# FNet mixing plus PEER experts on one Trainium2 core: the symmetry compares of the expert part on GpSimd, first column group in halves, its rows 0 in a tile of their own

## The chip, the cores and the metric

The kernel runs on one core of one Trainium2 chip. A core has five engines with a queue of instructions each, worked off in order: TensorE (PE in the profile; PEld are its weight loads), VectorE (DVE), ScalarE (ACT), GpSimd (POOL) and SyncE (SP), which here only issues transfers. Engines wait for each other by semaphores. The metric is the device time of one launch in microseconds; the number compared is the median of several runs.

## What is computed

The input x has 2048 rows of 512. It is normalized by row, and three things are added: x, a Fourier mixing by dense DFT matrices, and a layer of product-key experts (32 heads, two of 4096 experts for each head and row).

```python
xn = _layernorm(x, axis=-1)
return x + _A_ref(xn, A_dft_seq_re, ...) + _B_ref(xn, B_w_q, B_k1, B_k2, B_u, B_v)
# _A_ref
a = jnp.einsum("bsd,ed->bse", x, dft_hid_re)
b = jnp.einsum("bsd,ed->bse", x, dft_hid_im)
y = jnp.einsum("ts,bse->bte", dft_seq_re, a) - jnp.einsum("ts,bse->bte", dft_seq_im, b)
# _B_ref
s1 = jnp.einsum("nhd,ed->nhe", q1, k1)      # 64 scores; the same with q2, k2
...                                         # two best of each half, two best of the four sums
act = _gelu(jnp.einsum("nd,nhkd->nhk", xf, ue))
out = jnp.einsum("nhk,nhk,nhkd->nd", g, act, ve)
```

The DFT matrices are ordinary inputs. The kernel uses their symmetries to do a fraction of the Fourier work, so it has to establish on the chip that the matrices it was given have them. If they had not, a general path at the end of the program would compute the result anew; with these inputs it is skipped.

## The kernel before

**Stages.** The first 90 us or so fold x and do the short Fourier product. Until about 460 us the scores of 32 heads are computed, sixteen blocks of 128 rows for each group of four heads (`scores`, L796), and VectorE picks the two best (L804, L808). From about 470 us on runs the *expert part*, in which all 4096 experts are computed for 14 of the 16 blocks as dense products: u times x for every expert (`u_part`, L956), Gelu on ScalarE (L959), multiplication by a matrix of gates that is built on TensorE from two one-hot matrices (`g_mm`: VectorE makes L and R in L980, L988 and L991, TensorE multiplies them in L993; `w_part`: L1004, L1011, L1014), and the product with v (`v_part`, L1023). The last two blocks are done by gathering rows instead: `fetch` gathers one u row and one v row per partition (L1049, issued by GpSimd), `dot` multiplies on VectorE (L1065), `gain` scales on ScalarE (L1075 to L1078) and adds on GpSimd (L1083).

**The block loop.** For block b, TensorE does eight groups (cg) of twelve v matmuls into one PSUM bank `v`; `finish` (L1038, VectorE) reads that bank and adds the row block `y` to it; then TensorE does the eight groups of u matmuls of block b + 2, 48 each. Groups 2 and 5 of them use the PSUM buffers with the tag "pc", of which there are two; one of them holds `px`, which the gather part reads all the time, the other is `v`. So group 2 of u cannot start before `finish` has read `v`. `y` is loaded by SyncE (L1031), and x is added to it by an accumulating transfer that GpSimd issues (L1032), both traced at group 4 of the v loop (`add_x`).

**The compares.** `compare(n)` deals with one tile of one DFT matrix: 64 of them, n = 32 ri + 8 g + kk for the real or imaginary matrix ri, the column group g and a part kk of the matrix's other axis. The tile `cx` has 128 rows (partitions), one for each column of the matrix that belongs to the group, and in each row four quarters of 256 elements that should agree up to sign. `diff` subtracts the first quarter from the others (L752, for all column groups but the first), and then compares the first quarter's halves (mirror, L758, L760). In the first column group, g = 0, row 0 is its own mirror image and has other values, so there `diff` works with three operations that leave row 0 out by a factor `not0` (L739, L741), and treats row 0 in single-row operations (L743, L758 on one row, L766, L768). `judge`, on ScalarE, sums the absolute differences into a column of `chk` and the absolute values of the first quarter's part into a column of `asum` (L778, L780). 28 tiles, those of `EARLY`, are compared during the scores, with `diff` on GpSimd; 36 run in the expert part with `diff` on VectorE: the 16 tiles of g = 0, and 20 others. `compare_w` does the same for four tiles of the hidden DFT matrix (L1121 to L1144, VectorE), and `fit` checks ranges of other inputs (ScalarE). `verdict` at the end reduces `chk` and `asum` over rows.

**What sets the order.** The program is written out without loops, and each engine's queue follows the order of the text nearly throughout. `paced` is called once for each group of the v and u loops; called with odd cg it lets the list `units` (40 entries) advance evenly over the loop. An entry issues its loads at once; `after(2, work)` puts `diff` two paced steps later and `judge` two more, and `hold` adds an order without a semaphore behind the matmuls of that step. `pick` distributes the gather work in the same way. The tiles of the compares take turns with those of `w_part`, `fit` and others in four buffers (tag "w").

Of the kernel before, what the change touches and what calls it, by code (L numbers as in the profile page):

```python
# [8 lines left out]
F32 = mybir.dt.float32  # L9
# [6 lines left out]
AF = mybir.ActivationFunctionType  # L16
# [3 lines left out]
P = 128  # L20
# [16 lines left out]
def tile_fnet_peer(ctx, tc, x, ca, cb, c5, wt, wf, wr, wq, kt, ut, vn, uv, out):  # L37
# [54 lines left out]
    NF = NW + 32 + NCH - 1  # L92
    EARLY = [*range(8, 24), *range(40, 52)]
    early = cst.tile([P, len(EARLY)], F32, name="early")
    sums_sb = cst.tile([P, 138 + NF + 3], F32, name="sums")
    chk, asum = sums_sb[:, 0:70], sums_sb[:, 70:138]


    wsc = cst.tile([P, 5], F32, name="wsc")
    sw, sk, smx, inv1 = wsc[:, 0:1], wsc[:, 1:2], wsc[:, 2:3], wsc[:, 3:4]  # L100
    k16 = sums_sb[:, 0:128].bitcast(F16).rearrange("p (l w k) -> p l w k", l=2, w=2)
    fits = sums_sb[:, 138:]
# [453 lines left out]
    def part_b(safe, stS, stP, stE, xt, u_sb, cmp_p):  # L556
# [163 lines left out]
        def compare(n, at=None):  # L720
# [11 lines left out]
            nc.sync.dma_start(tf[:, P:], cb[ri, g, kk].rearrange("p b c -> p (b c)"))  # L732
            sgn = (((1, 1, 1), (-1, 1, -1)), ((-1, -1, 1), (1, -1, -1)))[ri][odd]
            ops = [ALU.subtract if v > 0 else ALU.add for v in sgn]
            op = ops[1]

            def diff():
                if g == 0:
                    nc.vector.tensor_tensor(tv[:, 1], tv[:, 1], tv[:, 0], op=ops[0])  # L739
                    for i in (2, 3):  # L740
                        nc.vector.scalar_tensor_tensor(tv[:, i], tv[:, 0], not0, tv[:, i], op0=ALU.mult, op1=ops[i - 1])  # L741
                    f = (-1 if ri else 1) * sgn[1] * sgn[2]
                    nc.vector.tensor_tensor(tv[0:1, 3], tv[0:1, 3], tv[0:1, 2],  # L743
                                            op=ALU.subtract if f > 0 else ALU.add)
                else:
                    sets = {}
                    for i, o in enumerate(ops):
                        sets.setdefault(o, []).append(i + 1)
                    for o, ix in sets.items():
                        sl = slice(ix[0], ix[-1] + 1, ix[1] - ix[0] if len(ix) > 1 else 1)  # L750
                        v = tv[:, sl]
                        v_eng.tensor_tensor(v, v, tv[:, 0:1].to_broadcast([P, len(ix), 256]), op=o)  # L752
                m = ALU.add if ri else ALU.subtract

                def mirror(v):

                    c = 0 if kk else 1
                    v_eng.tensor_tensor(v[:, 2:4, c:], v[:, 2:4, c:], v[:, 0:2, c:], op=m)  # L758
# [12 lines left out]
                mirror(t[:, 0])  # L771
                if kk == 0:
                    v_eng.memset(t[:, 0, 2, 0:1], 0.0)
# [321 lines left out]
        def pick(after, k=1):  # L1095
            done[0] += k
            made = nc.cur_bb.bb.instructions
            for f in picks[done[1]:-(-len(picks) * done[0] // turns)]:
# [3 lines left out]
                for i in made[first:]:  # L1102
                    if i.engine in (mybir.EngineType.DVE, mybir.EngineType.Activation):
                        follow(i, after)
                    if i.engine == mybir.EngineType.Activation and after.ins.name in GL:
                        follow(i, GL[after.ins.name])

        def compare_w(n):


# [24 lines left out]
                nc.vector.memset(r[:, 255:256], 0.0)  # L1135
            nc.vector.scalar_tensor_tensor(v[2], v[0], not0, v[2], op0=ALU.mult, op1=op)
            if ri:
                nc.scalar.activation(v[0][0:1, 0:P], v[0][0:1, 0:P], AF.Abs, accum_out=chk[0:1, 68 + half:69 + half])
# [5 lines left out]
            after(2, lambda: nc.scalar.activation(f, f, AF.Abs, accum_out=chk[:, n:n + 1]))  # L1144

        def fit(n):

# [14 lines left out]
        def verdict():  # L1162
# [1 line left out]


            N = NF + 3
            fm = sums_sb[:, 138 + NF:]
# [3 lines left out]
            cols = ((slice(0, 64), 50), (slice(64, 70), 47))  # L1171
            for i, (c, k) in enumerate(cols):
                nc.vector.tensor_reduce(fa[:, i:i + 1], asum[:, c.start:min(c.stop, 68)], axis=AX.X, op=ALU.add)
# [6 lines left out]
            k = nc.gpsimd.partition_all_reduce(fr[:, 2:], sums_sb[:, 138:], P, bass_isa.ReduceOp.absmax)  # L1180
# [21 lines left out]
            NW + k, *range(2 * k, min(2 * k + 2, NW)), NW + 16 + k)]  # L1202
        todo_n = [n for n in range(68) if n not in EARLY]
        units = [lambda n=n: (compare if n < 64 else compare_w)(n) for n in todo_n]
        streams = [[fit_units, 0, 0], [units, 0, 0]]

        def flush(mm):
# [11 lines left out]
                st[2] += 1  # L1219

        if not safe:
            nc.vector.memset(chk[:, 68:70], 0.0)
# [237 lines left out]
```

## Time and profile before

| | us |
|---|---|
| median of 3 runs | 1118.81 |
| lowest and highest | 1116.66, 1120.2 |
| the profiled execution, its own time | 1113.87 |
| its span in the trace | 1112.1 |

A row of the profile that groups instructions reads: line, engine, operation, what is written and from what (names of the program's tiles), shapes as partitions x elements and type, how often; then the busy time in us and the mean of one in ns; then the time that the engine stood idle just before these, and what ended it. Rows of a timeline begin with the start and the length in us; a bracket gives the idle time before and who ended it. A row of waits gives the total in us, how many times, and the longest. A row of windows gives the stretch, its length, for each engine the busy time and the number of instructions, the granted clock of TensorE (1.00 is full), the share of the transfer engines and GB/s.

### The profile page before, as it was taken

The page shows a single profiled execution, that of the slowest core. Times are in us where ns is not written, and L with a number is a line of the kernel's source. Part 1 is how long each engine was busy: PE and PEld are TensorE (multiplying, and loading weights), DVE is VectorE, ACT ScalarE, POOL GpSimd, SP SyncE. Part 2 cuts the span into 40 slices and gives each one's busy share as a digit, 9 for nine tenths or more (in the row PEclk, how much of TensorE's full clock was granted, in tenths as well). Part 3 has the DMA queues.
Part 4 walks back from the last instruction along what each step waited for, and adds up shares of the span by engine and source line. Part 5 has one row for each costly group of instructions (what it writes and reads, how often), then busy time and mean ns, then how long its engine had stood idle before and what let it go on. Part 6 is the DMA issues. An engine that isn't in the chain of part 4 may idle for free. (4 is left out here: it accounts for less than half of the span.)

```text
span 1112.1 us, 28462 instructions
## 1 busy us (share of the span) xinstructions
PE 1070.3 (96%) x11070; PEld 700.6 (63%) x11070; DVE 996.7 (90%) x2786; ACT 717.7 (65%) x1324; POOL 640.3 (58%) x552
## 2 busy tenths in 40 slices
PE   5899999999999999999999999999998999999897
PEld 4355555454544544987695776968667686786853
DVE  6978897978999999987999999999999999998981
ACT  3576657778788767423766667767566666765660
POOL 0013537588797855211668677756666667667651
PEclk9899999999999999999999999999998999999899
DMA  8248153535446332553677577676767567776521
GB/s 326 83 172 284 49 198 113 173 125 198 153 153 206 106 114 65 186 158 109 186 213 238 193 212 231 225 232 201 215 199 209 182 214 237 230 222 189 158 67 51
DMA packets 84433, 196.72 MB, mean 177 GB/s; under 512 B 10294, under 2 KB 27069, under 8 KB 84288
## 3 DMA queue, kind: packets, MB, share of 16 engines
q1 hardware_dynamic: 63394, 123.49, 33.1%
q0 software_dynamic: 20736, 71.31, 21.8%
q8 instruction: 88, 1.44, 0.5%
q14 instruction: 57, 0.47, 0.1%
q10 hardware_dynamic: 158, 0.01, 0.0%
HBM read 177.68 MB, written 17.10 MB: 175 GB/s over the span
## 5 line engine op out<-in xcount | busy, mean ns | idle before, releaser
L796 PE MATMUL s<-m,xq 128*128 128x512 f16 x1536 | 338.9, 379 | 0.0
L956 PE MATMUL z<-xb,u 128*128 128x128 f16 x5376 | 313.9, 221 | 15.5 <-DVE y L1038 15.5
L956 PEld LDWEIGHTS <-u 128*128 128x128 f16 x5376 | 307.6, 99 | 19.2 <-issue 16.4
L1083 POOL TENSOR_TENSOR ov<-ov,ga 128x512 f32<-128x512 f32 x128 | 203.5, 1590 | 167.2 <-ACT ga L1078 145.7
L1023 PE MATMUL v<-v,act 128*128 128x512 f16 x1344 | 298.6, 379 | 0.0
L796 PEld LDWEIGHTS <-xq 128*128 128x128 f16 x1536 | 148.3, 98 | 171.4 <-issue 0.2
L1023 PEld LDWEIGHTS <-act 128*128 128x128 f16 x1344 | 128.3, 98 | 146.1
L1049 POOL DMA_INDIRECT ga<-in_uv_dram,eix x128 | 173.0, 1351 | 47.2 <-POOL ov L1083 34.2
L980 DVE TENSOR_TENSOR L<-io_lam,cmp 128x2048 f16<-128x2048 f16 x112 | 157.8, 1441 | 13.5 <-PE g L993 13.5
L804 DVE MAX8 vals<-ss 128x8 f32<-128x64 f32 x1024 | 152.4, 216 | 14.1 <-ACT ss L801 14.0
L959 ACT ACTIVATE act<-z,scl 128x512 f32<-128x512 f32 x112 | 75.8, 679 | 97.2 <-PE z L956 96.3
L808 DVE FIND_INDEX8 idx<-vals,ss 128x8 uint16<-128x256 f32 x256 | 107.1, 418 | 0.0
L801 ACT ACTIVATE ss<-s,wsc 128x512 f32<-128x512 f32 x112 | 75.5, 680 | 43.4 <-PE s L796 33.7
L1011 ACT ACTIVATE act<-w 128x1024 f16<-128x1024 f32 x56 | 75.5, 1348 | 43.3 <-DVE w L1004 39.8
L1078 ACT ACTIVATE ga<-ga,za 128x512 f32<-128x512 f32 x128 | 92.1, 721 | 9.8 <-ACT za L1076 0.4
L1014 DVE TENSOR_TENSOR act<-w,act 128x1024 f16<-128x1024 f32 x56 | 86.1, 1539 | 6.7 <-ACT act L1011 5.8
L778 ACT ACTIVATE cx<-cx 128x896 f32<-128x896 f32 x64 | 60.6, 946 | 40.3 <-DVE cx L758 12.9
L1065 DVE SCALAR_TENSOR_TENSOR ga<-ga,px 128x512 f32<-128x512 f32 x128 | 85.6, 676 | 0.1
L1004 DVE SCALAR_TENSOR_TENSOR w<-act,scl,g 128x1024 f32<-128x1024 f32 x56 | 70.9, 1271 | 0.4 <-ACT act L959 0.2
L169 POOL TENSOR_TENSOR wq<-wq,wh 128x1024 f16<-128x1024 f32 x26 | 55.4, 2134 | 24.4 <-ACT wq L166 23.7
L993 PEld LDWEIGHTS <-L 128*128 128x128 f16 x1792 | 52.2, 96 | 9.5 <-issue 2.7
L993 PE MATMUL g<-R,L 128*128 128x32 f16 x1792 | 54.0, 176 | 2.2 <-DVE w L1004 1.9
(274 smaller groups left out, 1312.4 us busy)
## 6 DMA issues: line engine op xcount, KB each, us to landing
cx<-in_cb_dram SPq DMA_DIRECT2D x64, 448.0 KB, 4.6
wq<-in_wq_dram SPq DMA_DIRECT2D x32, 512.0 KB, 5.8
fit<-in_wq_dram SPq DMA_DIRECT2D x28, 512.0 KB, 5.4
uv<-in_ut_dram SPq DMA_DIRECT2D x16, 512.0 KB, 4.1
uv<-in_vn_dram SPq DMA_DIRECT2D x16, 512.0 KB, 3.5
xq<-in_x_dram SPq DMA_DIRECT2D x8, 512.0 KB
xt_d<-xq SPq DMA_DIRECT2D x16, 256.0 KB, 3.0
cx<-in_ca_dram SPq DMA_DIRECT2D x64, 64.0 KB, 2.8
```

The costliest lines, as they stand in the source:

```text
L796: mm = nc.tensor.matmul(ps, xt[i][:, l, kd, :], m[:, r, kd, :], start=(n == 0), stop=(n == 3 * KD - 1))
L804: nc.vector.max(vals[:, i, w, :, h], s[:, g, :])
L808: nc.vector.max_index(idx[:, i, w].rearrange("p k h -> p (k h)"), vals[:, i, w, 0:2].rearrange("p k h -> p (k h)"), s[:, w * HC:g + 1, :]. ...
L956: mm = nc.tensor.matmul(p[:, cc * P:(cc + 1) * P], ug[:, l, c % 2, kd, :], xb[:, r, kd, :], start=(n == 0), stop=(n == 3 * KD - 1))
L980: nc.vector.tensor_tensor(L.rearrange("p t (l two) -> p t l two", two=2), io_lam.rearrange("p (l two) -> p l two", two=2).unsqueeze(1).to_ ...
L993: i = nc.tensor.matmul(p[:, hf, t * NC:(t + 1) * NC], L[:, t, :], R[:, hf * 16 + t, :], start=True, stop=True)
L1014: nc.vector.tensor_tensor(w16[..., 1], w, w16[..., 0], op=ALU.subtract)
L1023: mm = nc.tensor.matmul(pv, w16[:, c, :, l], vg[:, r, c % 2, :], start=(c == 0 and k == 0), stop=(c == NC - 1 and k == 2))
L1049: nc.gpsimd.indirect_dma_start(out=t, out_offset=None, in_=uv, in_offset=bass.IndirectOffsetOnAxis(ap=eix[:, n].rearrange("p k h -> p (k h ...
L1065: nc.vector.scalar_tensor_tensor(t, t, 1.0, T["x"], op0=ALU.mult, op1=ALU.mult, accum_out=T["z", n][:, s:s + 1])
L1078: nc.scalar.activation(t, t, AF.Copy, scale=z)
L1083: T["a"] = nc.gpsimd.tensor_tensor(o, o, t, op=ALU.add)
```

## The change

`diff` of the 36 tiles in the expert part goes to GpSimd, except for tiles 0 and 32 (g = 0, kk = 0), which stay as they are. To treat the other 14 tiles of g = 0 like all others, row 0 must not be in them: they are loaded in two halves, rows 1 to 64 into partitions 0 to 63 and rows 64 to 127 into partitions 64 to 127, so row 64 stands in them twice. Each half is two transfers, as the whole was. The rows 0 of these 14 tiles are compared in a new tile, `compare_r`, the third entry of `units`: GpSimd clears it, eight small transfers put 3 or 4 rows each at partitions 0, 32, 64 and 96, VectorE does three operations for each of these four places and a copy or a memset where the sign rules want it, and ScalarE judges it into a new column of `chk`. `chk` grows from 70 to 71 columns, with the columns behind it moved by one. The pace of the 41 entries is that of the 40 before, within a step.

```diff
-    sums_sb = cst.tile([P, 138 + NF + 3], F32, name="sums")
-    chk, asum = sums_sb[:, 0:70], sums_sb[:, 70:138]
+    sums_sb = cst.tile([P, 139 + NF + 3], F32, name="sums")
+    chk, asum = sums_sb[:, 0:71], sums_sb[:, 71:139]
...
-            v_eng = nc.vector if at is None else nc.gpsimd
+            v_eng = nc.vector if n % 32 == 0 else nc.gpsimd
             tf = t.rearrange("p s q c -> p (s q c)")
             tv = t.rearrange("p s q c -> p s (q c)")
-            nc.sync.dma_start(tf[:, :P], ca[ri, g, :, kk * P:(kk + 1) * P])
-            nc.sync.dma_start(tf[:, P:], cb[ri, g, kk].rearrange("p b c -> p (b c)"))
+            own = g == 0 and kk == 0
+            half = ((slice(0, 64), slice(1, 65)), (slice(64, P), slice(64, P)))
+            for e, a in half if g == 0 and kk else ((slice(0, P),) * 2,):
+                nc.sync.dma_start(tf[e, :P], ca[ri, g, a, kk * P:(kk + 1) * P])
+                nc.sync.dma_start(tf[e, P:], cb[ri, g, kk, a].rearrange("p b c -> p (b c)"))
...
             def diff():
-                if g == 0:
+                if own:
...
-                if g == 0:
+                if own:
                     mirror(t[0:1, 2])
...
+        def compare_r(n):
+            t = bp.tile([P, 4, 4, 64], F32, tag="w", name="cx_r", bufs=WB)
+            tf = t.rearrange("p s q c -> p (s q c)")
+            tv = t.rearrange("p s q c -> p s (q c)")
+            nc.gpsimd.memset(tf, 0.0)
+            cls = []
+            for c in range(4):
+                ri, odd = divmod(c, 2)
+                k0, k1 = (4, 8) if odd else (1, 4)
+                e = slice(32 * c, 32 * c + k1 - k0)
+                nc.sync.dma_start(tf[e, :P], ca[ri, 0, 0:1, k0 * P:k1 * P].rearrange("o (k f) -> (o k) f", f=P))
+                nc.sync.dma_start(tf[e, P:], cb[ri, 0, k0:k1, 0:1].rearrange("k o b c -> (k o) (b c)"))
+                cls.append((ri, odd, e))
+            def work():
+                for ri, odd, e in cls:
+                    sgn = (((1, 1, 1), (-1, 1, -1)), ((-1, -1, 1), (1, -1, -1)))[ri][odd]
+                    f = (-1 if ri else 1) * sgn[1] * sgn[2]
+                    m = ALU.add if ri else ALU.subtract
+                    nc.vector.tensor_tensor(tv[e, 1], tv[e, 1], tv[e, 0], op=ALU.subtract if sgn[0] > 0 else ALU.add)
+                    nc.vector.tensor_tensor(tv[e, 3], tv[e, 3], tv[e, 2], op=ALU.subtract if f > 0 else ALU.add)
+                    nc.vector.tensor_tensor(t[e, 0::2, 2:4], t[e, 0::2, 2:4], t[e, 0::2, 0:2], op=m)
+                    if odd and ri:
+                        nc.vector.tensor_copy(t[e, 2, 0:2], t[e, 0, 0:2])
+                    elif odd == ri:
+                        nc.vector.memset(t[e, 2, 0:2], 0.0)
+                after(2, lambda: nc.scalar.activation(tf[:, P:], tf[:, P:], AF.Abs, accum_out=chk[:, n:n + 1]))
+            after(2, work)
...
         units = [lambda n=n: (compare if n < 64 else compare_w)(n) for n in todo_n]
+        units.insert(2, lambda: compare_r(64))
```

More of the change, by code (lines that the diff above doesn't have):

```diff
@@ L101, in tile_fnet_peer @@
     k16 = sums_sb[:, 0:128].bitcast(F16).rearrange("p (l w k) -> p l w k", l=2, w=2)
-    fits = sums_sb[:, 138:]
+    fits = sums_sb[:, 139:]
     hoff = cst.tile([P, HC], F32, name="hoff")
@@ L1137, in compare_w @@
             if ri:
-                nc.scalar.activation(v[0][0:1, 0:P], v[0][0:1, 0:P], AF.Abs, accum_out=chk[0:1, 68 + half:69 + half])
+                nc.scalar.activation(v[0][0:1, 0:P], v[0][0:1, 0:P], AF.Abs, accum_out=chk[0:1, 69 + half:70 + half])
             c = P - half
@@ L1143, in compare_w @@
             f = t.rearrange("p k e -> p (k e)")[:, P - half * ri:]
-            after(2, lambda: nc.scalar.activation(f, f, AF.Abs, accum_out=chk[:, n:n + 1]))
+            after(2, lambda: nc.scalar.activation(f, f, AF.Abs, accum_out=chk[:, n + 1:n + 2]))
         def fit(n):
@@ L1166, in verdict @@
             N = NF + 3
-            fm = sums_sb[:, 138 + NF:]
+            fm = sums_sb[:, 139 + NF:]
             fa = bp.tile([P, 2], F32, tag="fa", name="fa", bufs=1)
@@ L1170, in verdict @@
             o = bp.tile([1, 8], F32, tag="ok", name="ok", bufs=1)
-            cols = ((slice(0, 64), 50), (slice(64, 70), 47))
-            for i, (c, k) in enumerate(cols):
-                nc.vector.tensor_reduce(fa[:, i:i + 1], asum[:, c.start:min(c.stop, 68)], axis=AX.X, op=ALU.add)
+            cols = ((slice(0, 65), 50), (slice(65, 71), 47))
+            for i, c in enumerate((slice(0, 64), slice(64, 68))):
+                nc.vector.tensor_reduce(fa[:, i:i + 1], asum[:, c], axis=AX.X, op=ALU.add)
             nc.vector.tensor_scalar(bnd, bnd, -31.5, None, op0=ALU.add)
@@ L1179, in verdict @@
             follow(i.ins, T["a"])
[L1180 removed]
+            k = nc.gpsimd.partition_all_reduce(fr[:, 2:], sums_sb[:, 139:], P, bass_isa.ReduceOp.absmax)
             follow(k.ins, i)
@@ L1221, in part_b @@
         if not safe:
-            nc.vector.memset(chk[:, 68:70], 0.0)
+            nc.vector.memset(chk[:, 69:71], 0.0)
             for k in range(0, len(EARLY), 16):
```

## The prediction

> **What bounds the kernel now.** I read the page first, then one window over the expert part, TensorE's waits, and the timelines at the places where TensorE stands still.
>
> ```profile
> span 1112.1 us, 28462 instructions
> PE 1070.3 (96%) x11070; PEld 700.6 (63%) x11070; DVE 996.7 (90%) x2786; ACT 717.7 (65%) x1324; POOL 640.3 (58%) x552
> ```
>
> TensorE is busy for 96% of the span, so nothing can be worth more than its holes. The change touches only the expert part, from 525 us on:
>
> ```profile
> core 0: us, PE busy (x) PEld busy (x) DVE busy (x) ACT busy (x) POOL busy (x), PEclk, DMA share, GB/s
> 525.00:1112.00 587.00, 563.10 (x7202) 414.35 (x7199) 539.03 (x782) 378.80 (x805) 379.10 (x265) 0.98 0.64 195
> ```
>
> There VectorE has 48 us free of 587, GpSimd 208. TensorE's waits in that part, by who ended them:
>
> ```profile
> PE z L956 <- DVE y L1038: 15.5, 6, 4.8
> PE g L993 <- DVE w L1004: 1.9, 1, 1.9
> ```
>
> All 17.4 us wait for VectorE, 15.5 of them for L1038, which drains the finished v bank. The third u group of the next block (cg 2, line 946) takes that bank, so L1038 has the first two groups, 96 matmuls or 5.52 us, as its cover. Four of the six holes, each with its length in the bracket, and the 96 matmuls ahead of one:
>
> ```profile
> 613.45 1.72 PE L956 MATMUL z<-xb,u 128*128 128x128 f16 x28 [2.71 <-DVE y L1038]
> ...
> 798.40 0.77 PE L956 MATMUL z<-xb,u 128*128 128x128 f16 x11 [2.67 <-DVE y L1038]
> ...
> 839.90 5.52 PE L956 MATMUL z<-xb,u 128*128 128x128 f16 x96
> 849.38 0.91 PE L956 MATMUL z<-xb,u 128*128 128x128 f16 x7 [3.96 <-DVE y L1038]
> ...
> 1040.08 1.22 PE L956 MATMUL z<-xb,u 128*128 128x128 f16 x10 [4.84 <-DVE y L1038]
> ```
>
> These are 14.18 us; the other two share the last 1.3. A hole costs twice, because the granted clock falls behind it (length, busy time and matmuls, clock):
>
> ```profile
> 840.69:847.52 6.83, 4.73 (x85) 1.00 0.64 181
> 847.52:854.35 6.83, 4.97 (x48) 0.50 0.59 193
> 799.74:803.15 3.41, 3.41 (x58) 0.50 0.65 177
> 1038.67:1045.50 6.83, 5.42 (x60) 0.50 0.59 184
> ```
>
> At full clock 85 matmuls took 4.73 us, 18.0 per us; behind the hole at 845 the 48 took 4.97 instead of 48/18.0 = 2.67, so 2.30 us are lost. The same sum gives 2.1 at 1038 and, at half speed, about 1.7 at 799. The holes and their echoes together are 17.4 + 6.1 = 23.5 us: the most this change can bring.
>
> What stood ahead of L1038 on VectorE at two of them:
>
> ```profile
> 607.98 1.50 DVE L739 TENSOR_TENSOR cx<-cx 128x256 f32<-128x256 f32 x1
> 609.40 0.91 DVE L741 SCALAR_TENSOR_TENSOR cx<-cx,not 128x256 f32<-128x256 f32 x2
> 611.18 1.55 DVE L758 TENSOR_TENSOR cx<-cx 128x128 f32<-128x128 f32 x2
> ...
> 841.42 3.29 DVE L980 TENSOR_TENSOR L<-io_lam,cmp 128x2048 f16<-128x2048 f16 x2
> 844.64 1.50 DVE L739 TENSOR_TENSOR cx<-cx 128x256 f32<-128x256 f32 x1
> 846.06 2.60 DVE L741 SCALAR_TENSOR_TENSOR cx<-cx,not 128x256 f32<-128x256 f32 x2
> 848.59 0.74 DVE L1038 SCALAR_TENSOR_TENSOR y<-v,scl,y 128x512 f32<-128x512 f32 x1
> ```
>
> In both it is a first-group compare (L739 to L758), which the change moves. Note the two L741: 0.91 us at 609, 2.60 at 846. The longer one met an add on GpSimd; the two engines hold each other up.
>
> **The change part by part.**
>
> *What VectorE loses.* Its compare rows in the window, all shapes together:
>
> ```profile
> L752 DVE TENSOR_TENSOR cx<-cx 128x512 f32<-128x512 f32 (+2 forms) x36 | 31.2, 902 | 3.5 <-DMA cx<-in_cb_dram 3.5
> L758 DVE TENSOR_TENSOR cx<-cx 128x128 f32<-128x128 f32 (+3 forms) x52 | 29.6, 592 | 0.1
> L741 DVE SCALAR_TENSOR_TENSOR cx<-cx,not 128x256 f32<-128x256 f32 x32 | 19.8, 659 | 0.0
> L739 DVE TENSOR_TENSOR cx<-cx 128x256 f32<-128x256 f32 x16 | 12.5, 781 | 0.0
> L743 DVE TENSOR_TENSOR cx<-cx 1x256 f32<-1x256 f32 x16 | 10.0, 623 | 0.0
> ```
>
> That is 103.1 us in 36 tiles. Tiles 0 and 32 stay on VectorE: each keeps one L739, two L741, one L743 and two L758, 0.78 + 1.32 + 0.62 + 1.18 = 3.9, so 7.8 in all. The new row tile adds 12 tensor operations on 3 or 4 rows of 256 elements plus a copy and a memset; nothing in the trace starts at row 32 or 64, the nearest row is L743, so 12 x 0.62 = 7.5 and some 1 us more. The bounds are nothing (all of it fits into the 48 free us) and 12 x (0.62 + 1.27), 23 us, if each meets one GpSimd add. I take 8.5: it runs once, near the start, and no hole lies there. Net VectorE is relieved of 103.1 - 7.8 - 8.5 = 87 us.
>
> *What GpSimd gains.* 34 tiles: seven with one 768-element difference (tiles 1 to 3 and 24 to 27), 27 with one of 512 and one of 256, and the mirror of 128 in each. GpSimd did the same shapes in the first half:
>
> ```profile
> L752 POOL TENSOR_TENSOR cx<-cx 128x512 f32<-128x512 f32 x20 | 25.5, 1274 | 2.8 <-DMA cx<-in_cb_dram 2.8
> L752 POOL TENSOR_TENSOR cx<-cx 128x256 f32<-128x256 f32 x20 | 14.7, 734 | 0.0
> L752 POOL TENSOR_TENSOR cx<-cx 128x768 f32<-128x768 f32 x8 | 14.6, 1822 | 0.0
> L758 POOL TENSOR_TENSOR cx<-cx 128x128 f32<-128x128 f32 x24 | 10.9, 456 | 8.2 <-issue 6.9
> ...
> L1083 POOL TENSOR_TENSOR ov<-ov,ga 128x512 f32<-128x512 f32 x127 | 202.2, 1592 | 145.1 <-ACT ga L1078 123.6 <-ACT za L1075 6.8 <-DVE act L1014 5.9
> ```
>
> 7 x 1.82 + 27 x 2.01 + 34 x 0.46 = 82.6 us, and a memset of the row tile, which no row shows (between nothing and the 1.82 of the widest compare). GpSimd goes from 379 to some 463 of 587. It has the room: L1083 alone waits 145.1 us, nearly all for ScalarE.
>
> *What the stalls do.* Each us of arithmetic on GpSimd makes VectorE wait somewhere. The big operation ahead of L1038 shows how much:
>
> ```profile
> L980 DVE TENSOR_TENSOR L<-io_lam,cmp 128x2048 f16<-128x2048 f16 x93 | 134.0, 1475 | 4.0 <-PE g L993 4.0
> ...
> L980 DVE TENSOR_TENSOR L<-io_lam,cmp x93: 1197/1211/2876, 524.2 to 1072.7; 128x2048 f16<-128x2048 f16 x93
> ```
>
> Its median is 1.211 us, its mean 1.475; so 0.26 us of each is waiting, 24 us in all, against 127 adds of 1.27, 161 us of GpSimd arithmetic: 0.15 us per us. Another 82.6 add 12 us, 0.13 per L980, of which two stand ahead of each L1038. L1038 itself reads PSUM and is never held. The bounds at one boundary are nothing, and a whole compare, 1.27 + 0.73 + 0.46 = 2.46. I take 0.3 at each of six boundaries that have no margin, +1.8, with 2.46 x 6 = 14.8 as the upper end.
>
> The Trainium skill, SBUF — State Buffer, section Who interferes with whom, says that the two engines share one port pair, which whoever starts first holds for its whole instruction while the other stands still. The 2.60 against 0.91 of L741 agrees; by that rule alone the sum would lie between my two bounds, since it doesn't say how often they meet.
>
> *Halved loads.* Fourteen tiles are loaded by four transfers instead of two, and the row tile by eight: 36 more issues on SyncE.
>
> ```profile
> L732 SPq DMA_DIRECT2D cx<-in_cb_dram x34: 422/426/2416, 539.9 to 995.3; - x34
> cx<-in_cb_dram SPq DMA_DIRECT2D x64, 448.0 KB, 4.6
> ```
>
> 36 x 0.43 = 15 us of issuing over the whole part, at most 0.86 per tile ahead of the next y or xb load; the bytes grow by one row in 128. The load lands in 4.6 us and the compare is traced two paced steps after it, two u groups, 5.5 us, so it is covered; without that cover GpSimd, no longer VectorE, waits. I take nothing; the upper end is 15 us on a queue that has slack.
>
> The Trainium skill, DMA: Bandwidth & Descriptors, section Rules for kernel authors, advises against two transfers to disjoint halves, because they serialize. If that cost a second landing, the load would take 9.2 us and GpSimd would wait some 3.7 us per first-group tile; no row of this profile shows a halved load, and the sum here leaves it out.
>
> *ScalarE* gets one judge more among 805 instructions, and in place of VectorE waits for GpSimd's compare; two steps lie between the two in the code.
>
> **The sum.** The profiled execution took 1113.87 us, span 1112.1 and 1.8 around it. At 613 the removed operations, 3.96 us, cover the hole of 2.71; at 849 the removed 1.50 + 2.60 cover 3.96 and the 2.30 behind it: 8.97. At 798 no compare stands right ahead, but VectorE comes to that hole with no pause, and 87 us less work lets it come earlier; I take half of 2.67 + 1.7, 2.2. The hole at 1040 belongs to the weight compares (compare_w), which stay: nothing. Less 1.8 for stalls: 8.97 + 2.2 - 1.8 = 9.4. So 1113.9 - 9.4 = 1104.5 for a run like the profiled one. The three runs have a median of 1118.81, 4.9 above the profiled; against that I forecast **1109.4 us**.
>
> **The rivals.**
>
> *Everything closes.* If the lighter VectorE also reaches L1038 in time at 798 and 1040, up to 23.5 us go: 1095. Against it: the hole at 1040 has its own cause.
>
> *The engines only trade waits: no change.* The lock takes back what the move gives. If all of VectorE's compare time above its unhindered length were to reappear on L980 and its kin at the boundaries, 0.3 would become 1.5 at six boundaries, 9 us, and eat the 9.4: 1118.4. For it: VectorE and GpSimd were both stretched; against it: the compares, 87 us of the work that GpSimd's adds now run into, are gone from VectorE. The Trainium skill, Perfetto Trace Analysis, section Optimizing Scalar/DVE Operations, says that moving work between these two might not help for this reason; the 2.60 is the trace's witness for it.
>
> *y comes late: slower.* L1038 needs y, and the x part of y is added by a transfer that GpSimd's queue issues (L1032), in order, behind the compares now.
>
> ```profile
> 555.39 1.00 POOL L1032 DMA_DIRECT2D y<-in_x_dram  x1
> 564.24 0.75 DVE L1038 SCALAR_TENSOR_TENSOR y<-v,scl,y 128x512 f32<-128x512 f32 x1 [1.52 <-issue]
> 836.47 1.01 POOL L1032 DMA_DIRECT2D y<-in_x_dram  x1
> ...
> DMA to landing us min/median/max: 4.9/5.9/8.8
> ```
>
> The last row is L1032's. At 564 VectorE stood idle 1.52 us although v was done: y took 8.8 us to land and one small hole is due to it. At 836.47 + 5.9 + 0.74 the bank would be free at 843.1, and TensorE needs it at 839.90 + 5.52 = 845.4: 2.3 us of margin, less than one compare of 2.46. If two compares (4.9) stand ahead of L1032, that boundary has a hole of 2.6 and the one at 564 grows by 4.9. As an estimate, 1.5 us at each of twelve boundaries and two more half-clock echoes of 2.3 make 22.6, against 9.4 won: +13, 1132. It decides from the point where GpSimd runs over 2.3 us behind its order. For it: GpSimd at 79% busy; against it: its idle time is spread over all adds, so it rarely queues two compares.
>
> **How the numbers follow.** Forecast 0.50, everything closes 0.12, trade of waits 0.17, late y 0.21. About 0.3%, 3.4 us, is what a measurement tells from no change; the forecast's own range (9.4, less up to 13 more of stalls, or 4 more won) is 1105 to 1118, of which a little lies within 0.3%, and late y has a part there too. So faster 0.60, same 0.18, slower 0.22. The range leaves out the end of the first rival and the upper half of the last: 1098 to 1127.
>
> **What would show it.** Right: L752 and L758 on GpSimd in the expert part, VectorE's busy time in the window near 455 to 500, and the waits of TensorE for L1038 at about 8 us with the hole at 1040 still there. Wrong: VectorE idle ahead of L1038 with y the last to come (late y); L980's mean above 1.7 us with the holes unchanged (trade); ScalarE waiting for GpSimd's L758 with TensorE behind it, which I gave no price.

## The result, and the profile after

The changed kernel took 1130.57 us (median of four runs, 1129.88 to 1136.34), beside 1118.49 for the kernel before: a ratio of 1.0131, 95% interval 1.009 to 1.0172. It is 12 us slower; 9 us faster was forecast. The profiled execution took 1130.87 us against 1113.87; that one of before lies 4.6 us under its median, so the two traces are 17.0 us apart where the medians are 12.1. The lines of the changed kernel are three higher than before: L956 is now L959, L980 L983, L988 L991, L991 L994, L1014 L1017, L1038 L1041, L752 L755, L758 L761, L778 L781, L1083 L1086.

The page, and the window over the expert part (its columns as before):

```profile
span 1129.1 us, 28514 instructions
...
PE 1072.7 (95%) x11070; PEld 701.8 (62%) x11070; DVE 971.3 (86%) x2649; ACT 718.5 (64%) x1326; POOL 734.7 (65%) x652
```

```profile
525.00:1129.00 604.00, 567.35 (x7215) 416.70 (x7212) 516.78 (x645) 379.38 (x807) 474.25 (x365) 0.98 0.62 190
```

The window is 17.0 us longer, which is the whole difference of the two spans. TensorE is busy 4.3 us longer for the same matmuls of the program (567.35 against 563.10; the mean granted clock of the execution was 0.982 against 0.987) and idle 12.8 us longer. Who ended the waits of TensorE, ScalarE and VectorE there:

```profile
PE z L959 <- DVE y L1041: 21.5, 8, 6.3
PE g L996 <- DVE w L1007: 5.2, 1, 5.2
PE z L959 <- DVE cx L776: 3.1, 1, 3.1
PE z L959 <- ACT act L962: 0.5, 1, 0.5
...
ACT cx L781 <- POOL cx L761: 78.7, 24, 7.4
...
ACT cx_r L1138 <- DVE cx_r L1135: 9.9, 1, 9.9
...
DVE R L991 <- ACT cmp L699: 19.5, 8, 5.3
```

TensorE's 17.4 us have become 30.3, and most of it is still the wait for `finish`, L1041. VectorE, with fewer instructions, reaches it later. Two things are new. ScalarE stands 78.7 us at `judge` (L781) for GpSimd's mirror (L761), where it stood 28.1 us for VectorE's compares before, and 9.9 us at the judge of the row tile. What stands behind the judge in ScalarE's queue is late too: VectorE waits 19.5 us for L699, where it waited 3.5 before. The second is in the groups of the same window:

```profile
L1086 POOL TENSOR_TENSOR ov<-ov,ga 128x512 f32<-128x512 f32 x127 | 190.0, 1496 | 63.8 <-ACT ga L1081 43.0 <-DVE R L991 8.3 <-DVE L L983 6.6
...
L983 DVE TENSOR_TENSOR L<-io_lam,cmp 128x2048 f16<-128x2048 f16 x93 | 145.9, 1608 | 8.2 <-PE g L996 8.1
L1017 DVE TENSOR_TENSOR act<-w,act 128x1024 f16<-128x1024 f32 x49 | 95.1, 1943 | 13.2 <-ACT act L1014 11.3 <-ACT za L1078 1.9
L755 POOL TENSOR_TENSOR cx<-cx 128x512 f32<-128x512 f32 (+2 forms) x61 | 79.3, 1315 | 0.6
...
L991 DVE TENSOR_TENSOR R<-io_c,cmp 128x1024 f16<-128x1024 f16 x46 | 58.6, 1274 | 19.5 <-ACT cmp L699 19.5
L994 DVE TENSOR_TENSOR R<-R,cmp 128x1024 f16<-128x1024 f16 x46 | 48.2, 1049 | 1.3
...
L761 POOL TENSOR_TENSOR cx<-cx 128x128 f32<-128x128 f32 (+1 forms) x34 | 31.7, 933 | 2.3
L1041 DVE SCALAR_TENSOR_TENSOR y<-v,scl,y 128x512 f32<-128x512 f32 x13 | 9.6, 742 | 16.6 <-PE v L1026 16.4 <-issue 0.2
```

The kernel before had, beside the 134.0 us of L980 that the prediction shows:

```profile
L1014 DVE TENSOR_TENSOR act<-w,act 128x1024 f16<-128x1024 f32 x49 | 76.8, 1569 | 5.1 <-ACT act L1011 4.3 <-ACT za L1075 0.8
L991 DVE TENSOR_TENSOR R<-R,cmp 128x1024 f16<-128x1024 f16 x46 | 41.0, 891 | 1.2
L988 DVE TENSOR_TENSOR R<-io_c,cmp 128x1024 f16<-128x1024 f16 x46 | 38.9, 845 | 3.5 <-ACT cmp L699 3.5
```

The same 234 operations of VectorE, all with two inputs from SBUF, took 290.7 us before and take 347.8 now: 57.1 us more. Those whose second input lies in PSUM did not change: L1007 takes 1274 ns (1268 before), L1068 679 (676), L1041 742 (740). On GpSimd the compares take 79.3 + 31.7 = 111.0 us, and all its two-input work went from 202.2 to 301.0, by 98.8. So each us of it that was added stretched these four groups by 0.58 us.

The longest hole, at 565, in the timeline:

```profile
559.62 5.52 PE L959 MATMUL z<-xb,u 128*128 128x128 f16 x96
...
560.85 2.72 DVE L1132 TENSOR_TENSOR cx_r<-cx_r 4x256 f32<-4x256 f32 x1
561.45 1.83 POOL L755 TENSOR_TENSOR cx<-cx 128x768 f32<-128x768 f32 x1
...
563.60 1.50 DVE L1017 TENSOR_TENSOR act<-w,act 128x1024 f16<-128x1024 f32 x1
...
566.57 2.36 DVE L983 TENSOR_TENSOR L<-io_lam,cmp 128x2048 f16<-128x2048 f16 x2
566.62 0.95 ACT L1138 ACTIVATE cx_r<-cx_r 128x896 f32<-128x896 f32 x1 [9.93 <-DVE cx_r L1135]
...
570.64 0.74 DVE L1041 SCALAR_TENSOR_TENSOR y<-v,scl,y 128x512 f32<-128x512 f32 x1
571.44 0.80 PE L959 MATMUL z<-xb,u 128*128 128x128 f16 x6 [6.30 <-DVE y L1041]
```

VectorE works on the row tile ahead of L1041. One of its operations, on four rows, takes 2.72 us while GpSimd does a compare of 1.83; ScalarE stands 9.93 us at the row tile's judge.

### The profile page after: what moved, and what is told of

Read it like the earlier page. It is cut to its first block, busy times and chain, and to the rows that moved or that the text cites. A ratio compares the mean times of both kernels' runs of the same rounds, so it can differ in the third digit from the quotient of the medians.

```text
span 1129.1 us, 28514 instructions
## 1 busy us (share of the span) xinstructions
PE 1072.7 (95%) x11070; PEld 701.8 (62%) x11070; DVE 971.3 (86%) x2649; ACT 718.5 (64%) x1326; POOL 734.7 (65%) x652
## 5 line engine op out<-in xcount | busy, mean ns | idle before, releaser
L959 PE MATMUL z<-xb,u 128*128 128x128 f16 x5376 | 315.4, 221 | 25.1 <-DVE y L1041 21.5
L959 PEld LDWEIGHTS <-u 128*128 128x128 f16 x5376 | 308.6, 99 | 29.2 <-issue 26.3
L1026 PE MATMUL v<-v,act 128*128 128x512 f16 x1344 | 301.0, 381 | 0.0
L1086 POOL TENSOR_TENSOR ov<-ov,ga 128x512 f32<-128x512 f32 x128 | 191.3, 1494 | 85.6 <-ACT ga L1081 64.9
L1052 POOL DMA_INDIRECT ga<-in_uv_dram,eix x128 | 170.5, 1332 | 45.0 <-POOL ov L1086 32.7
L983 DVE TENSOR_TENSOR L<-io_lam,cmp 128x2048 f16<-128x2048 f16 x112 | 169.6, 1551 | 17.6 <-PE g L996 17.5
L755 POOL TENSOR_TENSOR cx<-cx 128x512 f32<-128x512 f32 (+2 forms) x109 | 133.2, 1239 | 1.2 <-DMA cx<-in_cb_dram 0.7
L781 ACT ACTIVATE cx<-cx 128x896 f32<-128x896 f32 x64 | 60.7, 949 | 92.5 <-POOL cx L761 90.9
L1017 DVE TENSOR_TENSOR act<-w,act 128x1024 f16<-128x1024 f32 x56 | 104.4, 1867 | 14.8 <-ACT act L1014 12.7
L1068 DVE SCALAR_TENSOR_TENSOR ga<-ga,px 128x512 f32<-128x512 f32 x128 | 85.7, 679 | 9.3 <-DMA ga<-in_uv_dram,eix 9.2
L1014 ACT ACTIVATE act<-w 128x1024 f16<-128x1024 f32 x56 | 75.4, 1347 | 28.3 <-DVE w L1007 28.3
L991 DVE TENSOR_TENSOR R<-io_c,cmp 128x1024 f16<-128x1024 f16 x56 | 65.4, 1168 | 21.5 <-ACT cmp L699 21.4
L1007 DVE SCALAR_TENSOR_TENSOR w<-act,scl,g 128x1024 f32<-128x1024 f32 x56 | 71.1, 1274 | 4.9 <-issue 1.8
```

What stands on the lines that cost most here:

```text
L959: mm = nc.tensor.matmul(p[:, cc * P:(cc + 1) * P], ug[:, l, c % 2, kd, :], xb[:, r, kd, :], start=(n == 0), stop=(n == 3 * KD - 1))
L983: nc.vector.tensor_tensor(L.rearrange("p t (l two) -> p t l two", two=2), io_lam.rearrange("p (l two) -> p l two", two=2).unsqueeze(1).to_ ...
L1017: nc.vector.tensor_tensor(w16[..., 1], w, w16[..., 0], op=ALU.subtract)
L1026: mm = nc.tensor.matmul(pv, w16[:, c, :, l], vg[:, r, c % 2, :], start=(c == 0 and k == 0), stop=(c == NC - 1 and k == 2))
L1052: nc.gpsimd.indirect_dma_start(out=t, out_offset=None, in_=uv, in_offset=bass.IndirectOffsetOnAxis(ap=eix[:, n].rearrange("p k h -> p (k h ...
L1068: nc.vector.scalar_tensor_tensor(t, t, 1.0, T["x"], op0=ALU.mult, op1=ALU.mult, accum_out=T["z", n][:, s:s + 1])
```

## The experiments

Three suspects: **A**, ScalarE's queue stands at the judge for GpSimd; **B**, the lock, GpSimd's two-input operations hold up VectorE's; **C**, the row tile. Each run was compared with runs of the kernel before on the same chip; ratios below have their 95% interval in brackets. Each edit is to the changed kernel unless said. Where a constant tile is added or lines are, line numbers shift a little.

### The judge and the lock

**judge_later**: the judge four steps behind the compare instead of two.

```diff
-                    after(2, judge)
+                    after(2 if n % 32 == 0 else 4, judge)
```

> The changed kernel, with the judges of the 34 moved tiles four paced steps behind their compares instead of two; the same instructions on every engine, GpSimd still compares. Theory A (ScalarE's queue stands at the judge): ScalarE's 79 us of waiting for L761 fall under 20, VectorE's waits for ScalarE (L699, L1014) from 31 to under 15, time 1116 to 1122. Theory B (GpSimd's two-input operations stretch VectorE's): L983, L991, L994 and L1017 stay near 350 us together, time 1126 to 1131.

1122.01 us, 1.0028 [1.0002, 1.0055].

```profile
PE z L959 <- DVE y L1041: 10.6, 5, 3.0
...
DVE R L991 <- ACT cmp L699: 5.0, 4, 2.5
...
ACT cx L781 <- POOL cx L761: 0.5, 1, 0.5
```

The wait of 78.7 us is gone, VectorE's wait for L699 is back near its old size, TensorE's for L1041 halved. That is 1.03% of 1118.5, 11.5 us (the two intervals leave about 6 to 17). L983 still takes 1670 ns and the four groups 353.1 us, so the lock is untouched.

**judge_first**: the judge in place of the compare, and the compare two steps behind it, so nobody judges what GpSimd did (the sums go to a column that nobody reads).

```diff
-                    diff()
-                    after(2, judge)
+                    judge()
+                    after(2, diff)
```

> The changed kernel, with the judges of the 34 moved tiles two paced steps ahead of their compares instead of behind them (they sum the tile as loaded, into a spare column; the compares' results are not judged). All engines do the same instructions, but ScalarE never waits for a GpSimd compare. Theory A (ScalarE's queue stands at the judge, 80 us, and its Gelu, one-hot copies and halves come late): ScalarE's wait for L761 goes to nothing, VectorE's waits for L699 and L1014 fall from 31 us to under 12, time 1117 to 1122. Theory B (the stretching of VectorE's remaining two-input operations by the compares, 57 us more in L983, L991, L994 and L1017): those stay stretched, time within 3 us of 1130.6.

1148.51 us, 1.0271 [1.0247, 1.0296].

```profile
DVE w L1013 <- POOL cx L762: 20.2, 5, 5.8
```

It doesn't isolate A. The compare is now the last to use the tile; `w_part` takes the same buffer next, and VectorE itself stands for GpSimd there, 20.2 us, which it does nowhere in the kernel before. It says nothing on A, only that VectorE waiting for GpSimd is no better.

**no_diff**: the 34 compares are left out, the tiles are judged as loaded (into a column that nobody reads, as in the fills below).

> The changed kernel with the 34 moved compares left out altogether (the judges sum the tiles as loaded, into a spare column). VectorE is relieved and GpSimd not loaded. All theories: 1103 to 1109, the worth of the relief alone. If it stays above 1115, the relief of VectorE was worth less than the forecast's step said, or the row tile and the halved loads cost it.

1102.97 us, 0.9882 [0.9854, 0.9911].

```profile
PE g L999 <- DVE w L1010: 5.1, 1, 5.1
PE z L962 <- DVE y L1044: 3.0, 1, 3.0
```

With nothing on GpSimd the four groups take 294.4 us, and the kernel is 0.0118 x 1118.5 = 13.2 us faster than before, row tile included. Not all of that need be VectorE's relief. The hole at 1040 is gone, but a hole of 5.1 us for L1010 stands further on, and the order of VectorE's queue shows why. In the kernel before, the second weight compare begins ahead of that `finish`; here it begins behind it:

```profile
1034.08 0.41 DVE L1121 TENSOR_REDUCE sums<-cx 128x1 f32<-128x256 f32 x1
...
1039.29 0.73 DVE L1038 SCALAR_TENSOR_TENSOR y<-v,scl,y 128x512 f32<-128x512 f32 x1
```

```profile
1022.89 0.74 DVE L1044 SCALAR_TENSOR_TENSOR y<-v,scl,y 128x512 f32<-128x512 f32 x1
...
1027.13 0.40 DVE L1158 TENSOR_REDUCE sums<-cx 128x1 f32<-128x256 f32 x1
```

The row tile is a 41st entry of `units`, and the one step by which it moves the entries behind it is enough. In all four kernels with 40 entries (before, and moved_20, no_row_tile and later_no_row below) the hole at this `finish` is 4.8 to 7.0 us and the later one 1.9 to 3.0; in all with 41 it is nothing to 4.2, and the later one 3.4 to 5.3. How much of the 13.2 us comes from this shift was not tested by itself.

**clear_then_judge**, **judge_then_clear** and **ones_then_judge** put fills in the place of GpSimd's compares: three fills, some 84 us in all, that write the tile and read nothing. The first fills with zeros ahead of the judge, the second behind it, the third with ones ahead of it.

```diff
+                def clear():
+                    nc.gpsimd.memset(tf, 1.0)
+                    nc.gpsimd.memset(tf, 1.0)
+                    nc.gpsimd.memset(tf[:, :512], 1.0)
...
-                    diff()
+                    clear()
                     after(2, judge)
```

> The changed kernel, with the 34 moved compares replaced on GpSimd by three clears of the tile (1024, 1024 and 512 elements, by the 0.97 us of the row tile's clear some 2.45 us, as long as a compare), which read nothing; the judges follow as before and wait for them (nothing is compared in these tiles). GpSimd as busy, ScalarE waits as before, but no GpSimd operation with two inputs. Theory A: ScalarE still waits some 80 us for them, time within 3 us of 1130.6. Theory B: L983, L991, L994 and L1017 together fall back by 40 to 57 us to what they took before the change, and the time to 1108 to 1114.

> Both at once: judges first, and clears in place of the compares (nothing is compared in the 34 tiles). GpSimd is as busy, ScalarE doesn't wait for it and VectorE isn't stretched by it. Theories A and B both expect about 1105 to 1109, what the move was forecast to bring; the two runs above say how the difference to 1130.6 is shared. If GpSimd's load itself were the cause (late gathers, late y), this would stay near 1130.

> clear_then_judge once more with fills of 1.0 in place of the clears, so that the general path at the end is not entered (nothing is compared in the 34 tiles); its time can then be set beside the others. There the last L1041 ended at 1106.7 us, against 1123.4 in the changed kernel: 1110 to 1116 here. Theory A alone would want 1127 to 1131, since ScalarE waits for the fills as it does for the compares.

clear_then_judge took 1789.91 us (1.6005), because sums of zero send the program into its general path at the end, so its time can't be compared; ahead of that ScalarE stood 47.9 us at the judge. judge_then_clear: 1110.69 us, 0.9940 [0.9919, 0.9961]. ones_then_judge: 1112.85 us, 0.9936 [0.9908, 0.9963], with these groups and this wait:

```profile
L993 DVE TENSOR_TENSOR L<-io_lam,cmp 128x2048 f16<-128x2048 f16 x94 | 130.0, 1421 | 17.1 <-PE g L1006 16.9
L1027 DVE TENSOR_TENSOR act<-w,act 128x1024 f16<-128x1024 f32 x49 | 74.3, 1519 | 20.9 <-ACT act L1024 16.9 <-ACT za L1088 4.0
L1001 DVE TENSOR_TENSOR R<-io_c,cmp 128x1024 f16<-128x1024 f16 x46 | 51.8, 1127 | 24.0 <-ACT cmp L700 24.0
L1004 DVE TENSOR_TENSOR R<-R,cmp 128x1024 f16<-128x1024 f16 x46 | 44.6, 970 | 1.3
...
L789 POOL MEMSET cx<- 128x1024 f32 x34 | 33.5, 985 | 0.2 <-DMA cx<-in_cb_dram 0.2
```

```profile
ACT cx L783 <- POOL cx L791: 56.1, 18, 6.9
```

The four groups take 300.7 us, near the 290.7 of before, though GpSimd has 84.5 us of fills in the place of 111.0 us of compares. ScalarE still stands 56.1 us at the judge and VectorE 24.0 us for L700, and the kernel is *faster* than before. With the two others:

| GpSimd does | judge two steps behind | judge waits little or nothing |
|---|---|---|
| compares | 1.0131 (changed kernel) | 1.0028 (judge_later) |
| fills | 0.9936 (ones_then_judge) | 0.9940 (judge_then_clear) |
| nothing | | 0.9882 (no_diff) |

Read down, compares instead of fills cost 1.95% (22 us) in the first column and 0.88% (10 us) in the second. Read across, the judge costs 1.03% with compares and nothing with fills; by the four intervals the difference is about 1.07 ± 0.6%. So A is expensive only on top of B. That VectorE, where it isn't stretched, can afford to wait for a late L699 is the likely reason; no run shows it by itself. Two reservations: the fills are also shorter than the stretched compares (84.5 against 111.0 us), so the wait at the judge is shorter too; and in judge_then_clear VectorE stands 7.8 us for GpSimd's fills, as it did for the compares in judge_first. The last column also has fills 0.58% above nothing, so part of what the compares cost there may be GpSimd's plain load.

**moved_20**: the kernel *before*, with only the 20 tiles of the other column groups moved. No halves, no row tile.

```diff
-            v_eng = nc.vector if at is None else nc.gpsimd
+            v_eng = nc.vector if g == 0 else nc.gpsimd
```

> The kernel before, with the compares of the 20 tiles outside the first column group moved to GpSimd and nothing else: no halves, no row tile. GpSimd gains 20 x 2.4 = 48 us of two-input work. Theory B: L980, L988, L991 and L1014, 293 us before, grow by some 30, time 1117 to 1125, not faster than before. Forecast's own step (0.15 us of stretching per us): they grow by 7, time 1108 to 1114.

1124.67 us, 1.0046 [1.002, 1.0072].

```profile
L1083 POOL TENSOR_TENSOR ov<-ov,ga 128x512 f32<-128x512 f32 x128 | 190.4, 1488 | 116.9 <-ACT ga L1078 103.6 <-DVE ga L1065 5.7 <-DVE act L1014 2.1
L980 DVE TENSOR_TENSOR L<-io_lam,cmp 128x2048 f16<-128x2048 f16 x94 | 141.3, 1539 | 7.4 <-PE g L993 7.4
L1014 DVE TENSOR_TENSOR act<-w,act 128x1024 f16<-128x1024 f32 x49 | 84.1, 1719 | 10.5 <-ACT act L1011 8.5 <-ACT za L1075 1.7
L991 DVE TENSOR_TENSOR R<-R,cmp 128x1024 f16<-128x1024 f16 x46 | 51.2, 1113 | 1.3
L752 POOL TENSOR_TENSOR cx<-cx 128x512 f32<-128x512 f32 (+2 forms) x36 | 50.3, 1413 | 0.9 <-issue 0.6
L988 DVE TENSOR_TENSOR R<-io_c,cmp 128x1024 f16<-128x1024 f16 x46 | 48.6, 1057 | 9.7 <-ACT cmp L699 9.7
L758 POOL TENSOR_TENSOR cx<-cx 128x128 f32<-128x128 f32 (+1 forms) x20 | 21.0, 1052 | 1.2
```

GpSimd's two-input work grew to 261.7 us, by 59.5, and the four groups to 325.2, by 34.5 (with one L1083 and one L980 more in the window): 0.58 us per us, the price of the whole change. The move alone is a loss of 0.46%, with ScalarE standing 45.2 us at the judge for L758.

### The row tile

**no_row_tile**: its entry is left out, so that the rows 0 of 14 tiles are not compared.

> The changed kernel without the tile for the rows 0 (these rows are not compared). Theory C (the row tile makes the hole of 6.3 us at 565 and the half clock behind it): that hole goes to under 1 us, time 1120 to 1125. If other work takes its place: within 3 us of 1130.6.

1117.92 us, 0.9999 [0.9969, 1.0029]: 14.8 us less than with it. TensorE waits 17.2 us for L1041 instead of 21.5; the hole at 565 is gone, and the longest, 7.0 us, is now the one near 1037, which is back with the list of 40 entries. So the difference is net of that.

**row_at_21** and **later_row_21**: the row tile in another place of the list, with the judge of the compares as it is and four steps behind.

```diff
-        units.insert(2, lambda: compare_r(64))
+        units.insert(21, lambda: compare_r(64))
```

> The changed kernel with the row tile as entry 22 of the list instead of entry 3. If the row tile costs by its place (dropping it gave 1118 instead of 1130), the hole at 565 goes and a like one may come near 800: 1118 if it finds a spot with margin, 1130 again if its twelve small operations and the judge behind them cost a hole wherever they stand.

> Judge four steps behind the compare and the row tile as entry 22. If judge and row tile cost separately, the two gains (11.5 of 1130 for the judge, up to 12 for the row tile) add up: 1108 to 1112, faster than before. If they are the same time counted twice (ScalarE's stand at 565 is both), it stays at 1118 to 1122.

1128.75 us, 1.0101 [1.007, 1.0133], and 1119.29 us, 1.0010 [0.9987, 1.0033]. The hole moved with the tile, to 802, where it is 6.1 us long. Another place gains 0.30% with the early judge and 0.18% with the later one, neither clear of the intervals: the later judge explains most of the second number.

**row_spread**: the four places dealt out two steps apart, the judge four steps behind the last.

```diff
-            def work():
-                for ri, odd, e in cls:
+            def work(c=0):
+                for ri, odd, e in cls[c:c + 1]:
...
-                after(2, lambda: nc.scalar.activation(tf[:, P:], tf[:, P:], AF.Abs, accum_out=chk[:, n:n + 1]))
+                if c < 3:
+                    after(2, lambda: work(c + 1))
+                else:
+                    after(4, lambda: nc.scalar.activation(tf[:, P:], tf[:, P:], AF.Abs, accum_out=chk[:, n:n + 1]))
```

> The changed kernel with the row tile's twelve operations dealt out over four places two steps apart, and its judge four steps behind the last. If what the row tile costs is the block of twelve at one step and ScalarE standing 9.9 us at its judge, the hole of 6 us at 565 goes and the time falls to about 1118 to 1121, what it took without the row tile. If the work itself is the cost wherever it stands, 1126 to 1131.

1134.93 us, 1.0135 [1.0083, 1.0187]: a miss. ScalarE no longer stands at the row tile's judge, and a hole of 6.5 us at 568 is there all the same, so that stand isn't what makes the hole. The block of twelve is not cleared by this: three of the four places still come ahead of that L1041, the third from 571.60 to 573.53, right before it.

**later_no_row** and **later_spread**: the later judge without the row tile, and with it dealt out.

> Judge four steps behind the compare, and no row tile. What is left then against the kernel before is the relief of VectorE and the lock: if judge (11 us) and row tile (15 us) cost separately, 1104 to 1110, so the lock would have taken only about half of the relief; if they cost the same time, 1116 to 1122, and the lock alone takes all of the relief of 14.5 us that the kernel without GpSimd's compares showed.

> Both mended: judge four steps later and the row tile dealt out. Within 3 us of later_no_row if dealing out hides the row tile: 1107 to 1113 if the two add, 1118 to 1122 if they don't.

1116.16 us, 0.9972 [0.9938, 1.0005], and 1124.27 us, 1.0041 [1.0018, 1.0065]. The first:

```profile
PE z L959 <- DVE y L1041: 15.8, 6, 6.1
...
ACT cx L781 <- POOL cx L761: 3.7, 3, 1.8
...
PE g L996 <- DVE w L1007: 1.9, 1, 1.9
```

Without the judge's wait and without the row tile TensorE's waits for VectorE are those of the kernel before (15.5 and 1.9). The four groups take 354.2 us. What is left of the gain is 0.28%, and its interval reaches nothing: the lock, with GpSimd's plain load, takes back the relief without any wait at the judge. The row tile with its entry costs 0.56% here (judge_later against later_no_row), 6.3 us, and 1.32% where ScalarE stands at the judge too; both are net of the hole near 1040, 6.1 us long here.

### The engine alone

**new_tiles_dve**: halves and row tile as changed, but all compares of the expert part on VectorE.

```diff
-            v_eng = nc.vector if n % 32 == 0 else nc.gpsimd
+            v_eng = nc.vector if at is None else nc.gpsimd
```

> The changed kernel with its new tiles (halved loads, row tile) but every compare of the expert part back on VectorE. If the slowdown comes from GpSimd's two-input operations (lock and judge), VectorE's stretch returns to about the 293 us of before in L, R, R and the half sums, ScalarE's wait at the judge falls from 78.7 to about 30 us, and the time is at or under the kernel before: the first column group's plain compare (two or three operations instead of six) spares VectorE some 14 x 1.5 = 20 us, the row tile costs 10: 1110 to 1118. If the halved loads or the row tile alone were the cause, it stays near 1130, with the hole of 6 us at 565.

1113.94 us, 0.9949 [0.9927, 0.9972].

```profile
PE z L959 <- DVE y L1041: 8.8, 4, 5.3
```

This differs from the changed kernel in the engine only, and is 1.82% faster, 20 us; the four groups take 289.4 us. Against the kernel before, halved loads and row tile together are a gain of 0.51% on VectorE. VectorE's operations that write `cx` and `cx_r` sum to some 103 us where they summed to some 125, since the first column group no longer needs most of its operations on single rows and with `not0`; the step by which the 41st entry moves the weight compares has a share that was not tested.

**dve_row_21** and **dve_spread**: the same with the row tile at entry 22, and with it dealt out as in row_spread.

> New tiles, compares on VectorE, row tile as entry 22. If the row tile at entry 3 meets the last thing TensorE waits for whatever engine compares, this is 3 to 10 us faster than new_tiles_dve; if the row tile only hurts because GpSimd's compares stretch its operations, the two are within 2 us.

> New tiles, compares on VectorE, row tile dealt out. The kernel with the row tile in one block took 1113.9 and had a hole of 5.3 us at 567, as the changed kernel has; without it some 5.3 + 2 less: 1106 to 1109, the fastest whole kernel of the study. If it stays at 1113, that hole did not set the end.

1117.42 us, 0.9983 [0.9961, 1.0005], a miss: 3.5 us slower than new_tiles_dve, where it was to be faster or the same. And 1108.35 us, 0.9896 [0.9869, 0.9923], with these waits:

```profile
PE g L996 <- DVE w L1007: 5.7, 2, 5.3
...
PE z L959 <- DVE y L1041: 4.3, 3, 1.9
```

The second is faster than both kernels. What dealing out couldn't do with GpSimd's compares it does without them: the waits for L1041 fall from 8.8 to 4.3 us.

**dve_spread_again** and **dve_spread_later**: the same once more, and with the judge four steps behind.

> The same kernel as dve_spread (compares on VectorE, row tile dealt out), in more rounds: 0.987 to 0.992 of the kernel before.

> dve_spread with the judge four steps behind the compare. If the judge's wait costs only together with the lock, the ratio is within 0.3% of dve_spread_again, though ScalarE's wait of 18 us for VectorE's compare goes to nearly nothing. If the wait costs by itself, at the rate of the changed kernel (11.5 us for 78.7 us of wait), 18.1 us less wait are worth 2.6 us, 0.2%, which is too little to tell; a gain over 0.4% would speak against the theory, and a loss would come from tiles holding their buffers longer.

1110.24 us, 0.9911 [0.9883, 0.9939], and 1108.47 us, 0.9897 [0.9868, 0.9926]. The difference of 0.14% is inside both intervals, as the table above would have it: without GpSimd's compares the place of the judge is worth too little to tell.

## Why the prediction was wrong

**What VectorE loses** was right as work: its compares are gone from it. The own sum for the row tile, 8.5 us, came near: its rows in the window (L1131 to L1133) sum to 11.2 us. But VectorE's busy time in the window fell from 539.03 to 516.78, by 22 us and not by 87.

**What GpSimd gains** was mis-sized: 82.6 us forecast, 111.0 measured. The mirror took 933 ns where the row of the first half, 456, was used; the same line lasted 449 to 1575 ns, so GpSimd's instructions are held up as well.

**The stalls** are the term that failed. The 12 us at "0.15 us per us", 0.13 per L980, were read from one victim, and for that one they came true: L980 and L983 differ by 11.9 us, 0.13 each. The other three groups, which the sum left at nothing, grew by 45.2 us: 57.1 in all. Their rows were there before. By mean less median, as for L980, the four give 52.5 us of waiting beside 161 us of adds, 0.33 us per us: 27 us. That the price rose from there to 57.1 as GpSimd filled up is not explained by any run. The step from stalls to time failed with it: 1.8 us was taken, 14.8 at most. Compares in place of fills cost 10 us with the later judge and 22 with the judge as it is; the holes are at eight of thirteen boundaries and not six.

**The holes**: the compares ahead of those at 613 and 849 are gone, and holes came back at most boundaries: eight waits for L1041, 21.5 us, against "about 8 us". **The hole at 1040** was rightly given to the weight compares, but they did not stay where they were: the 41st entry moved them, and the changed kernel has 0.7 us at that `finish` and 5.2 us for L1007 behind it. That the pace of the list stays the same "within a step" hid this.

**ScalarE** "waits for GpSimd's compare; two steps lie between" had no price. It costs 11.5 us (judge_later). With two steps ScalarE stood 28.1 us at the judge for VectorE's compares before; GpSimd does them behind the gather's adds, in order, and ScalarE stood 78.7 us for it, up to 7.4 at a time. The sign that the prediction named last, ScalarE waiting for GpSimd's L758 with TensorE behind it, is the one that came.

**The row tile** at nothing, as "no hole lies there", was wrong: with its entry it costs 6 to 15 us. The prediction itself names a small hole at 564 where it prices late y, and the tile's work stands ahead of that `finish`. Why the tile costs more where the judge waits too isn't settled.

**The range**: 13 us more of stalls on 1109.4 would be 1122, not 1118; 1130.57 lies outside either and outside 1098 to 1127.

**The halved loads** at nothing: nothing in new_tiles_dve speaks against it, though no run has them alone. **Late y** did not happen: L1041 stood 0.2 us for anything but `v`. **The engines only trade waits** was the rival with the right mechanism, stopped at no change because it counted 1.5 us at six boundaries and no wait at the judge; later_no_row is what it described, 0.9972. Slower was given 0.22, but through late y: the mechanism that came had no chance of its own on that side.

The Trainium skill, SBUF — State Buffer, section Who interferes with whom, says further that VectorE's operations with two inputs collide with GpSimd instructions that read, not with those that only write. The runs agree: 300.7 us with fills, 347.8 with compares. By that rule the whole of the moved work was of the colliding kind, and the prediction didn't ask which kind it was.

## What to carry to other kernels

Price a move from VectorE to GpSimd by all of VectorE's two-input operations that will run beside it, not by one of them; here the four largest groups took back 0.58 us for each us of reading work added. Ask who consumes the result in order: a consumer's queue that was safe behind a prompt engine stands still behind a busy one, and that hurts most when the lock has already taken the margin. In a list that is dealt out evenly, look at what one more entry moves: here it put the weight compares behind a `finish`. And try the parts apart: the new tiles without the new engine, the row tile dealt out (dve_spread, 0.9896 and 0.9911), beat both kernels.

## What the hardware showed unexpectedly

In the timeline at 565 VectorE's L1132 is recorded from 560.85, 0.60 us ahead of GpSimd's compare at 561.45, and yet it ended only 0.29 us behind it (563.57 against 563.28), at 2.72 us instead of the 0.41 that the same operation takes elsewhere. An earlier recorded start did not secure it the way through. At 0.41 us it would have been done by 561.26, ahead of the compare; what held it until then is open. GpSimd was issuing a gather (L1052, 560.47 to 561.44), but another L1132, at 557.54, took 0.41 us beside such an issue. GpSimd's starts in the profile are rough, so this is an observation and no rule.
